# Linear attention and SwiGLU on one core: opening batch in token halves, row transposes by DMA, casts on ScalarE, loads in order of need

## The chip, the cores and the metric

The kernel runs on one core of a Trainium2 chip. The metric is the device time of the whole program in microseconds (us), as the median of several executions. A profile is one execution with the hardware profiler on. Its span runs from the first to the last instruction and is some 2 us shorter than the time.

Names of the engines in the profile: PE is TensorE's matmuls, PEld its weight loads, DVE is VectorE, ACT is ScalarE, POOL is GpSimd, SPq and ACTq are the sequencers of SyncE and ScalarE while they issue DMAs. PSUM is the memory in which the matmuls of these kernels leave their results.

## The reference, cut to what matters

```python
def _attn_ref(q, k, v, g_norm):                 # 8 batches, 8 heads, 576 tokens, 64 per head
    kv = np.einsum('bhsd,bhse->bhde', k, v)
    out = np.einsum('bhsd,bhde->bhse', q, kv)
    rms = np.sqrt(np.mean(out * out, axis=-1, keepdims=True) + 1e-06)
    return out / rms * g_norm

def _moe_ref(x, w_gate, w_val, w_out, rms_g):   # x: 4608 tokens x 512; d_ff = 1536
    rms = np.sqrt(np.mean(x * x, axis=-1, keepdims=True) + 1e-06)
    xn = x / rms * rms_g
    g = xn @ w_gate
    return (g / (1 + np.exp(-g)) * (xn @ w_val)) @ w_out
```

The first function feeds the second: its output, with the heads side by side, is `x`. The softmax is absent, so a whole batch needs only one 64x64 matrix per head, but all of K and V must have been seen before the first output exists.

## The kernel before

Both kernels work through nine groups of 512 tokens. Groups 0 to 7 are the first 512 tokens of each batch; group 8 holds the eight tails of 64 tokens. In a group there are 12 "up" units (four gate and four value matmuls of 128x512, then silu on ScalarE and the product `h` on VectorE) and four "down" units of 12 matmuls each. The attention of the next batch is put between these units by hand; the program order on each engine is the order in which the lines are issued.

Two normalisations are folded into one factor `alpha` per token and head. It needs two sums of squares per head, one plain and one weighted with the gains, and an inverse square root made by two Newton steps on VectorE ("the chain"). The gains go into the FFN weights when these are rounded to bf16.

The parts that the change touches:

```python
        def sums(self, c):                       # for each 128 tokens: VectorE
            nc.vector.tensor_tensor(out=wsq, in0=self.sq, in1=gsq8, op=OP.mult)
            nc.vector.reduce_sum(out=self.ssq[:, c, :], in_=self.sq, axis=AX.X)
            nc.vector.reduce_sum(out=self.wssq[:, c, :], in_=wsq, axis=AX.X)

        def xT(self, pair):                      # rows -> columns on TensorE, then a PSUM copy
            ...
                    nc.tensor.matmul(ps[:, j, i, :], lhsT=self.xna[2 * pair + i][:, 2 * j : 2 * j + 2, :],
                                     rhs=identity, is_transpose=True, ...)
            nc.vector.tensor_copy(out=xnts[self.n][:, :, 256 * pair : 256 * pair + 256], in_=...)
    ...
    round_main(0, "k", nc.gpsimd)                # the opening: all of batch 0 first
    round_main(0, "v", nc.vector)
    round_main(0, "q", nc.scalar)
    att = Att(0)
    att.kv(); att.qT(0); att.qT(1)               # (one call per line in the kernel)
    for c in range(T):
        att.o(c)
        att.sums(c)
    att.chain_a(); att.chain_b()
    ...                                          # scale, transpose
    for blk in range(NF // JB):
        load_w12(blk)
        round_w12(blk, "g", nc.gpsimd)
        round_w12(blk, "v", nc.gpsimd)
    ...
    for n in range(B + 1):
        ...
                12: [lambda: nxt.xT(0), lambda: nxt.scale(2), lambda: nxt.scale(3)],
                13: [lambda: nxt.xT(1)],
        for unit in range(NF + T):
            if unit < NF:
                ffn.up(unit)
                if n == 0 and unit == NF - 1:    # all of w_out is rounded before the first down unit
                    for blk in range(NF // JB):
                        round_wo(blk, nc.vector if blk % 2 else nc.scalar)
            else:
                ffn.down(unit - NF)
            for step in steps.get(unit, []):
                step()
```

Of the kernel before, what the change touches and what calls it, by code (L numbers as in the profile page):

```python
# [17 lines left out]
def kernel(  # L18
# [22 lines left out]
    HALF_B = B // 2  # L41
    NS = d_model // 128
    NF = d_ff // 128
    JB = 2
    assert TAIL == 64 and B * TAIL == MAIN and 2 * D == 128

    consts = ctx.enter_context(tc.tile_pool(name="consts", bufs=1))
    qkv_pool = ctx.enter_context(tc.tile_pool(name="qkv", bufs=2))
    stage_pool = ctx.enter_context(tc.tile_pool(name="stage", bufs=8))
    raw_pool = ctx.enter_context(tc.tile_pool(name="raw", bufs=3))  # L50
    qt_pool = ctx.enter_context(tc.tile_pool(name="qt", bufs=2))
    outa_pool = ctx.enter_context(tc.tile_pool(name="outa", bufs=6))
    sq_pool = ctx.enter_context(tc.tile_pool(name="sq", bufs=3))
    xna_pool = ctx.enter_context(tc.tile_pool(name="xna", bufs=4))
    stat_pool = ctx.enter_context(tc.tile_pool(name="stat", bufs=2))
    xnt_pool = ctx.enter_context(tc.tile_pool(name="xnt", bufs=2))
    h_pool = ctx.enter_context(tc.tile_pool(name="hsb", bufs=1))
    silu_pool = ctx.enter_context(tc.tile_pool(name="silu", bufs=3))
    osb_pool = ctx.enter_context(tc.tile_pool(name="osb", bufs=3))

    gps_pool = ctx.enter_context(tc.tile_pool(name="gps", bufs=2, space=bass.MemoryType.PSUM))
    vps_pool = ctx.enter_context(tc.tile_pool(name="vps", bufs=2, space=bass.MemoryType.PSUM))
    ops_pool = ctx.enter_context(tc.tile_pool(name="ops", bufs=2, space=bass.MemoryType.PSUM))
    att_pool = ctx.enter_context(tc.tile_pool(name="att", bufs=2, space=bass.MemoryType.PSUM))
# [4 lines left out]
    def main_view(x, b):  # L69
        return x[b, :, 0:MAIN, :].rearrange("h (p t) d -> p h (t d)", t=T)  # L70

    def tail_view(x, b0, b1):
        return x[b0:b1, :, MAIN:S, :].rearrange("b h r d -> r (b h) d")



    k_tail = consts.tile([128, HALF_B, H, D], BF16, name="k_tail")
    q_tail = consts.tile([128, HALF_B, H, D], BF16, name="q_tail")
    v_tail = consts.tile([128, B, H, D], BF16, name="v_tail")

    def load_tails(x, dst, b0, b1):
        u = b0 // HALF_B
        cols = slice(b0, b1) if dst is v_tail else slice(b0 - u * HALF_B, b1 - u * HALF_B)
        nc.gpsimd.dma_start(
            out=dst[u * TAIL : (u + 1) * TAIL, cols].rearrange("r b h d -> r (b h) d"),
            in_=tail_view(x, b0, b1),
        )

    batches = {}
    raws = {}  # L90

    def load_main(b):
        for name, src in (("k", k), ("v", v), ("q", q)):
            st = raw_pool.tile([128, H, T * D], FP32, name="raw")
            nc.sync.dma_start(out=st, in_=main_view(src, b))  # L95
            raws[b, name] = st

    def round_main(b, name, engine):
        t = qkv_pool.tile([128, T, H, D], BF16, name=name + "_t")
        for hh in range(2):  # L100
            hs = slice(hh * H // 2, (hh + 1) * H // 2)
            dst = t[:, :, hs, :].rearrange("p t h d -> p h t d")
            src = raws[b, name][:, hs, :].rearrange("p h (t d) -> p h t d", t=T)
            if engine is nc.scalar:
                engine.copy(out=dst, in_=src)
            else:
                engine.tensor_copy(out=dst, in_=src)  # L107
        batches.setdefault(b, {})[name] = t


    gcol = consts.tile([128, 1], FP32, name="gcol")
    gview = g_norm.rearrange("(d o) -> d o", o=1)
    nc.sync.dma_start(out=gcol[0:D], in_=gview)
    nc.sync.dma_start(out=gcol[D : 2 * D], in_=gview)
    rmsg_sb = consts.tile([128, NS], FP32, name="rmsg_sb")
    nc.sync.dma_start(out=rmsg_sb, in_=moe_rms_g.rearrange("(s p) -> p s", p=128))
    gnorm_bc = consts.tile([128, D], FP32, name="gnorm_bc")
    nc.sync.dma_start(out=gnorm_bc, in_=g_norm.partition_broadcast(128))

    load_main(0)  # L120
    nc.vector.memset(k_tail, 0.0)
    nc.vector.memset(v_tail, 0.0)
    load_tails(k, k_tail, 0, 1)
    load_tails(v, v_tail, 0, 1)

    identity = consts.tile([128, 128], BF16, name="identity")
    make_identity(nc, identity)

    kv_all = consts.tile([128, B, NS, 2, D], BF16, name="kv_all")
    nc.vector.memset(kv_all, 0.0)  # L130

    rowscale = consts.tile([128, NS], FP32, name="rowscale")
    nc.vector.tensor_scalar(
        out=rowscale, in0=rmsg_sb, scalar1=gcol[:, 0:1], scalar2=None, op0=OP.mult
    )
    gsq8 = consts.tile([128, H, D], BF16, name="gsq8")
    nc.vector.tensor_tensor(
        out=gsq8[:, 0, :], in0=gnorm_bc, in1=gnorm_bc, op=OP.mult
    )
    for n in (1, 2, 4):  # L140
        nc.vector.tensor_copy(out=gsq8[:, n : 2 * n, :], in_=gsq8[:, 0:n, :])

    qt_tail = consts.tile([128, HALF_B, 2, NS, 128], BF16, name="qt_tail")


    wg_sb = consts.tile([128, NS, d_ff], BF16, name="wg_sb")
    wv_sb = consts.tile([128, NS, d_ff], BF16, name="wv_sb")
    wo_sb = consts.tile([128, NF, d_model], BF16, name="wo_sb")
    wg_view = moe_w_gate.rearrange("(s p) f -> p s f", p=128)
# [3 lines left out]
    w_stages = {}  # L153

    def load_w12(blk):
        cols = slice(blk * JB * 128, (blk + 1) * JB * 128)
        for name, view in (("g", wg_view), ("v", wv_view)):
            st = stage_pool.tile([128, NS, JB * 128], FP32, name="w_st")
            nc.sync.dma_start(out=st, in_=view[:, :, cols])
            w_stages[name, blk] = st  # L160

    def round_w12(blk, name, engine):
        dst = {"g": wg_sb, "v": wv_sb}[name]
        for s in range(NS):
            engine.tensor_scalar(  # L165
                out=dst[:, s, blk * JB * 128 : (blk + 1) * JB * 128], in0=w_stages[name, blk][:, s, :],
                scalar1=rowscale[:, s : s + 1], scalar2=1.0, op0=OP.mult, op1=OP.mult,
            )

    def load_wo(blk):  # L170
        st = stage_pool.tile([128, JB, d_model], FP32, name="w_st")
        nc.sync.dma_start(out=st, in_=wo_view[:, blk * JB : (blk + 1) * JB, :])
        w_stages["o", blk] = st

    def round_wo(blk, engine):
        dst = wo_sb[:, blk * JB : (blk + 1) * JB, :]
        if engine is nc.scalar:
            engine.copy(out=dst, in_=w_stages["o", blk])  # L178
        else:
            engine.tensor_copy(out=dst, in_=w_stages["o", blk])  # L180


    xnts = {}

    class Att:



        def __init__(self, n):
            self.n = n  # L190
            self.tail = n == B

        def kv(self):
            n, t = self.n, batches[self.n]
            ps = att_pool.tile([128, NS, 2 * D], FP32, name="att_ps")
            for j in range(NS):
                for c in range(T + 1):
                    if c < T:
                        kk, vv = t["k"][:, c, 2 * j : 2 * j + 2, :], t["v"][:, c, 2 * j : 2 * j + 2, :]
                    else:  # L200
                        kk, vv = k_tail[:, n % HALF_B, 2 * j : 2 * j + 2, :], v_tail[:, n, 2 * j : 2 * j + 2, :]
                    nc.tensor.matmul(  # L202
                        ps[:, j, :], lhsT=kk, rhs=vv,
                        start=(j == 0 and c == 0), stop=(j == NS - 1 and c == T),
                    )
            nc.vector.tensor_copy(out=kv_all[0:D, n, :, 0, :], in_=ps[0:D, :, 0:D])
            nc.vector.tensor_copy(out=kv_all[D:128, n, :, 1, :], in_=ps[D:128, :, D : 2 * D])

        def qT(self, pair):
            ps = att_pool.tile([128, 2, NS, 128], BF16, name="att_ps")  # L210
            for i in range(2):
                c = 2 * pair + i
                for j in range(NS):
                    src = q_tail[:, c, 2 * j : 2 * j + 2, :] if self.tail else (
                        batches[self.n]["q"][:, c, 2 * j : 2 * j + 2, :])
                    nc.tensor.matmul(  # L216
                        ps[:, i, j, :], lhsT=src, rhs=identity, is_transpose=True,
                        start=(i == 0 and j == 0), stop=(i == 1 and j == NS - 1),
                    )
            if self.tail:  # L220
                for i in range(2):
# [81 lines left out]
        def xT(self, pair):  # L303
            if pair == 0:
                xnts[self.n] = xnt_pool.tile([128, NS, MAIN], BF16, name="xnt")
# [87 lines left out]
    for n in range(B + 1):  # L393
# [8 lines left out]
        if n + 2 < B:  # L402
            load_main(n + 2)
# [74 lines left out]
```

## Time and profile before

The median of the first three runs is 398.69 us (397.28 to 400.91). The best ruler for this kernel is the start of the first gate matmul of each group, read from the timeline of PE:

| stage (before) | from | to | us |
|---|---|---|---|
| opening | 0 | 41.84 | 41.8 |
| group 0 | 41.84 | 95.70 | 53.9 |
| group 1 | 95.70 | 136.56 | 40.9 |
| groups 2 to 7 | 136.56 | 362.39 | 225.8 |
| group 8 and the last stores | 362.39 | 398.2 | 35.8 |

(The prediction has 42.8 and 96.5 for the first two borders: the first gate matmuls of these groups stand apart from the next by a gap, 0.22 us in group 0, and I had cut after them.)

The page of the kernel before, parts 1 and 2: busy time of each engine, then PE's busy share and the granted TensorE clock in 40 slices of 10 us, each digit in tenths.

```profile
PE 331.8 (83%) x1868; PEld 167.0 (42%) x1904; DVE 208.5 (52%) x443; ACT 145.1 (36%) x247; POOL 81.0 (20%) x107
...
PE   0231890897998999899989998998999899989995
...
PEclk9999996896998999999989999999999999989999
```

PE is busy 83% of the span, and the first four slices hold little (9.15 us of the first 41.84, by the windows view): the opening is not bound by TensorE. The view of waits, PE's own: what it waited for, total, number of times, longest.

```profile
PE att_ps L309 <- DVE xna L298: 28.7, 18, 11.9
...
PE att_ps L202 <- DMA v_tail<-in_v_dram: 9.6, 1, 9.6
```

The longest of the first, 11.9 us, is the sums and the chain of the opening; the 9.6 us is one load in group 0. The timeline of PE (start, duration, engine, line, operation, output from inputs, array tile, size, count, and in brackets the idle time before with its releaser) shows that load, and the start of group 0:

```profile
41.84 0.58 PE L329 MATMUL g_ps<-xnt,wg_sb 128*128 128x512 bf16 x1 [0.78 <-DVE xnt L314]
...
43.51 1.91 PE L335 MATMUL v_ps<-xnt,wv_sb 128*128 128x512 bf16 x4
45.21 1.08 PE L329 MATMUL g_ps<-xnt,wg_sb 128*128 128x512 bf16 x4
...
69.02 0.27 PE L202 MATMUL att_ps<-v_tail,k_tail 128*128 128x128 bf16 x1 [9.56 <-DMA v_tail<-in_v_dram]
```

Finally the windows view for a steady group: the window, its length, then busy time and number of instructions of PE, PEld, DVE, ACT and POOL, the granted clock, the DMA share, GB/s.

```profile
212.45:249.57 37.12, 35.02 (x210) 17.83 (x212) 22.30 (x48) 15.25 (x26) 6.08 (x6) 1.00 0.35 115
```

Of 37.12 us PE is busy 35.0, and 35.0 is more than the 31.1 us that the FFN's 144 matmuls of 0.216 us need: attention and its transposes take the rest.

### The profile page before, as it was taken

What the parts mean: (1) busy time and instruction counts of PE and PEld (TensorE: products, weight loads), DVE (VectorE), ACT (ScalarE), POOL (GpSimd) and SP (SyncE); (2) the same over time, 40 slices, a digit from 0 to 9 for tenths busy, and PEclk for the clock granted to TensorE, in tenths of its full rate; (3) what the DMA queues carried; (4) which work ended last, traced back from release to release, by engine and by line L of the source; (5) the groups of instructions that cost most, each with busy time, mean ns of one, the idle gap of its engine ahead of it and who ended that gap; (6) DMA issues with size and microseconds to landing.
All of it is one profiled execution on the core that took longest, in us unless ns stands there. A gap on an engine that the chain in (4) does not pass through costs nothing.

```text
span 398.2 us, 4990 instructions
## 1 busy us (share of the span) xinstructions
PE 331.8 (83%) x1868; PEld 167.0 (42%) x1904; DVE 208.5 (52%) x443; ACT 145.1 (36%) x247; POOL 81.0 (20%) x107
## 2 busy tenths in 40 slices
PE   0231890897998999899989998998999899989995
PEld 0220440543543454355435544543454345434442
DVE  5268330395568157716852784388257815761320
ACT  1170130561551265136413631462255136412321
POOL 2299945600500032005100500050000000000000
PEclk9999996896998999999989999999999999989999
DMA  5999999817400290057005701740110020002004
GB/s 143 344 348 348 365 247 213 53 54 225 146 0 0 95 323 8 0 172 251 2 24 173 228 1 54 239 132 0 68 39 1 2 105 2 0 2 105 0 14 93
DMA packets 49145, 45.97 MB, mean 115 GB/s; under 512 B 14305, under 2 KB 45025, under 8 KB 49121
## 3 DMA queue, kind: packets, MB, share of 16 engines
q1 hardware_dynamic: 36704, 44.08, 34.5%
q0 software_dynamic: 12416, 1.57, 6.1%
q8 instruction: 15, 0.25, 0.2%
q14 instruction: 10, 0.07, 0.1%
HBM read 37.78 MB, written 9.44 MB: 119 GB/s over the span
## 4 chain that ended last, share of the span: by engine, by line
PE 63%; DVE 15%; DMA 9%; POOL 7%; issue 3%; SPq 2%; ACT 1%; DVEq 0%; ACTq 0%; POOLq 0%
PE o_ps L346 19%; PE v_ps L335 18%; PE g_ps L329 18%; DMA v_tail<-in_v_dram 6%; DVE h_sb L341 4%; POOL wg_sb L165 3%; POOL wv_sb L165 3%; DMA w_st<-in_moe_w_gate_dram 3%; DVE xna L298 3%; PE att_ps L202 2%; PE att_ps L309 2%; PE att_ps L243 2%; PE att_ps L216 2%; DVE ssq L257 1%; SPq L95 1%
## 5 line engine op out<-in xcount | busy, mean ns | idle before, releaser
L341 DVE TENSOR_TENSOR h_sb<-silu,v_ps 128x512 bf16<-128x512 bf16 x108 | 73.9, 685 | 123.3 <-PE v_ps L335 117.6
L329 PE MATMUL g_ps<-xnt,wg_sb 128*128 128x512 bf16 x414 | 111.2, 385 | 2.6 <-DVE xnt L314 1.6
L335 PE MATMUL v_ps<-xnt,wv_sb 128*128 128x512 bf16 x425 | 112.0, 384 | 0.6
L346 PE MATMUL o_ps<-wo_sb,h_sb 128*128 128x512 bf16 x421 | 101.8, 393 | 1.9 <-ACT wo_sb L178 1.3
L340 ACT ACTIVATE silu<-g_ps 128x512 bf16<-128x512 f32 x108 | 65.2, 603 | 103.3 <-PE g_ps L329 97.1
L335 PEld LDWEIGHTS <-wv_sb 128*128 128x128 bf16 x432 | 42.7, 99 | 52.7 <-issue 2.7
L346 PEld LDWEIGHTS <-h_sb 128*128 128x128 bf16 x432 | 42.8, 101 | 52.2 <-issue 8.1
L352 ACT COPY o_sb<-o_ps 128x512 f32<-128x512 f32 x36 | 21.1, 586 | 102.6 <-PE o_ps L346 102.4
L329 PEld LDWEIGHTS <-wg_sb 128*128 128x128 bf16 x432 | 40.8, 99 | 41.7 <-issue 4.1
L107 POOL CAST k_t<-raw 128x1024 bf16<-128x1024 f32 x16 | 16.5, 1062 | 160.9 <-DMA raw<-in_k_dram 123.3
L309 PE MATMUL att_ps<-identity,xna 128*128 128x128 bf16 x144 | 14.7, 240 | 28.7 <-DVE xna L298 28.7
L248 ACT ACTIVATE sq<-att_ps 128x512 bf16<-128x512 f32 x36 | 21.8, 605 | 14.0 <-PE att_ps L243 14.0
L309 PEld LDWEIGHTS <-xna 128*128 128x128 bf16 x144 | 9.6, 105 | 37.3 <-DVE xna L298 35.5
L202 PE MATMUL att_ps<-v_t,k_t 128*128 128x128 bf16 x128 | 11.6, 239 | 15.5 <-DVE v_t L107 15.5
L257 DVE TENSOR_REDUCE ssq<-sq 128x8 f32<-128x512 bf16 x36 | 24.4, 677 | 0.0
L258 DVE TENSOR_REDUCE wssq<-wsq 128x8 f32<-128x512 bf16 x36 | 24.3, 674 | 0.0
L314 DVE COPY xnt<-att_ps 128x1024 bf16<-128x1024 bf16 x18 | 12.4, 691 | 18.0 <-PE att_ps L309 17.9
L250 ACT CAST outa<-att_ps 128x512 bf16<-128x512 f32 x36 | 21.2, 588 | 0.0
L228 ACT COPY qt<-att_ps 128x1024 bf16<-128x1024 bf16 x16 | 16.1, 1013 | 11.4 <-PE att_ps L216 11.4
L256 DVE TENSOR_TENSOR wsq<-sq,gsq_137 128x512 bf16<-128x512 bf16 x36 | 17.1, 476 | 5.2 <-ACT sq L248 5.2
L202 PEld LDWEIGHTS <-k_t 128*128 128x128 bf16 x128 | 10.1, 108 | 21.0 <-POOL k_t L107 12.4
L107 POOL CAST q_t<-raw 128x1024 bf16<-128x1024 f32 x14 | 14.2, 1045 | 7.5 <-DMA raw<-in_q_dram 5.0
(85 smaller groups left out, 192.8 us busy)
## 6 DMA issues: line engine op xcount, KB each, us to landing
raw<-in_k_dram SPq DMA_DIRECT2D x8, 1024.0 KB, 7.1
raw<-in_v_dram SPq DMA_DIRECT2D x8, 1024.0 KB, 9.6
raw<-in_q_dram SPq DMA_DIRECT2D x8, 1024.0 KB, 11.7
out_dram<-o_sb SPq DMA_DIRECT2D x16, 512.0 KB, 2.9
w_st<-in_moe_w_gate_dram SPq DMA_DIRECT2D x6, 512.0 KB, 8.9
w_st<-in_moe_w_val_dram SPq DMA_DIRECT2D x6, 512.0 KB, 8.8
w_st<-in_moe_w_out_dram SPq DMA_DIRECT2D x6, 512.0 KB, 10.3
out_dram<-o_sb SPq DMA_DIRECT2D x8, 128.0 KB, 2.3
```

The costliest lines, as they stand in the source:

```text
L107: engine.tensor_copy(out=dst, in_=src)
L165: engine.tensor_scalar(out=dst[:, s, blk * JB * 128 : (blk + 1) * JB * 128], in0=w_stages[name, blk][:, s, :], scalar1=rowscale[:, s : s + ...
L202: nc.tensor.matmul(ps[:, j, :], lhsT=kk, rhs=vv, start=(j == 0 and c == 0), stop=(j == NS - 1 and c == T),)
L248: nc.scalar.activation(out=sq, in_=ps, func=ACT.Square)
L257: nc.vector.reduce_sum(out=self.ssq[:, c, :], in_=self.sq, axis=AX.X)
L258: nc.vector.reduce_sum(out=self.wssq[:, c, :], in_=wsq, axis=AX.X)
L309: nc.tensor.matmul(ps[:, j, i, :], lhsT=self.xna[2 * pair + i][:, 2 * j : 2 * j + 2, :], rhs=identity, is_transpose=True, start=(i == 0 an ...
L329: nc.tensor.matmul(g_ps, lhsT=wg_sb[:, s, j * 128 : (j + 1) * 128], rhs=x[:, s, :], start=(s == 0), stop=(s == NS - 1),)
L335: nc.tensor.matmul(v_ps, lhsT=wv_sb[:, s, j * 128 : (j + 1) * 128], rhs=x[:, s, :], start=(s == 0), stop=(s == NS - 1),)
L340: nc.scalar.activation(out=silu, in_=g_ps, func=ACT.Silu)
L341: nc.vector.tensor_tensor(out=self.h[:, j, :], in0=silu, in1=v_ps, op=OP.mult)
L346: nc.tensor.matmul(o_ps, lhsT=self.h[:, j, c * 128 : (c + 1) * 128], rhs=wo_sb[:, j, :], start=(j == 0), stop=(j == NF - 1),)
```

## The change

Its intent: the opening should reach the FFN sooner, and a steady group should hold fewer TensorE instructions and no wait for the rows of the next group.

- Batch 0 is worked in two halves of 256 tokens. Its sums of squares are small matmuls against a four-column matrix `sel` (a plain and a weighted sum for each of two heads), and its chain has 12 operations, not 16. Group 0 starts on the first half.
- The transposes of `q` and of the normalised rows, from batch and group 2 on, are `dma_start_transpose` on SyncE's queue; they were TensorE matmuls plus PSUM copies. Batch 1 keeps TensorE.
- The casts to bf16 in steady groups go from GpSimd to ScalarE; the weight rounding from GpSimd to ScalarE (gate) and VectorE (value).
- The tails of K and V are plain loads with a cast, no longer casting DMAs of GpSimd. Loads are issued in the order of need; seven stage buffers are shared.
- The rounding of `w_out` moves into the down part of group 0, block by block.

The diff cut to its core (cuts marked):

```diff
+    def chain(u, w, nc_, name):                 # 11 operations, and one before it
+        ...
+        nc.vector.scalar_tensor_tensor(out=z, in0=m.to_broadcast(shape), scalar=eps, in1=u, ...)
+        ...
+        def x_rows(self, c):
+            nc.sync.dma_start_transpose(
+                out=xnts[self.n][:, :, 128 * c : 128 * c + 128],
+                in_=self.xna[c].rearrange("p h d -> p (h d)"),
+            )
...
-    round_main(0, "k", nc.gpsimd)
-    round_main(0, "v", nc.vector)
-    round_main(0, "q", nc.scalar)
-    att = Att(0)
-    ...
+    A, Bh = Open(0), Open(1)                    # the two halves
+    for j in range(NS):                         # per pair of heads
+        cast_piece(0, "k", j, nc.vector)
+        cast_piece(0, "v", j, nc.scalar)
+        ps = att_pool.tile([128, 128], FP32, name="att_ps")
+        warm(ps, 3, 128)                        # three dummy matmuls
+        for c in range(T + 1):
+            nc.tensor.matmul(ps, lhsT=kbs[0][:, c, hs, :], rhs=vbs[0][:, c, hs, :], ...)
+        nc.vector.tensor_copy(out=kv_all[0:D, 0, j, 0:D], in_=ps[0:D, 0:D])
+        nc.vector.tensor_copy(out=kv_all[D:128, 0, j, D:128], in_=ps[D:128, D:128])
+        A.outT(j)                               # one matmul of 128x256
+        A.square(j)                             # ScalarE
+    A.sums(); A.o(); ...; A.chain(); ...        # (one call per line in the kernel)
+    ffn.up(0, 0, 256)
+    Bh.chain()
+    ...
+    ffn.up(3, 0, 256)
+    for j in range(4):
+        ffn.up(j, 256, 512)                     # the second half of units 0 to 3
+        ...
+    for j in range(4, NF):
+        ffn.up(j)
+        ...
+    att.kv_products((0, 1))                     # batch 1, in the down part of group 0
+    att.kv_products((2, 3))
+    att.kv_copy()
+    for blk in range(3):
+        round_wo(blk, 0, nc.scalar)
+        round_wo(blk, 1, nc.vector)
+        if blk == 0:
+            for i in range(4):
+                cast_piece(1, "q", i, nc.scalar if i % 2 else nc.vector)
+        for c in range(2):
+            ffn.down_products(c, 4 * blk, 4 * blk + 4)
+        if blk == 0:
+            att.q_turn(0, nc.scalar)
+        if blk == 1:
+            att.q_turn(1, nc.vector)
+            att.o(0)
+            att.sums(0)
+        if blk == 2:
+            att.o(1)
+            att.sums(1)
+    ...
+    ffn.down_products(3, 0, NF)
+    att.x_turn(0, nc.vector)
+    att.x_turn(1, nc.vector)
+    ffn.down_out(3)
+    for n in range(1, B + 1):                   # the other groups
+        ...
```

## The prediction

> **What bounds the kernel now.** The span is 398.2 us. In the chain of waits TensorE (PE) has 63%. The windows view, cut at the first gate matmul of each token group: opening with group 0, 96.5 us; group 1, 40.0; groups 2 to 7, 37.1 to 38.8 (226.0 together); tail group 8 with the last stores, 35.7.
> In the first 42.8 us PE is busy only 9.9 us. The timeline shows why: K, V, Q land at 11.3, 14.7, 17.7 us; all of batch 0 is finished before the first FFN matmul; sums and the Newton chain keep VectorE from 23 to about 37 us; GpSimd rounds weights until 43.8. Then PE waits 9.6 us for v_tail (waits view), a cast DMA behind GpSimd work.
> A steady group is 31.1 us of FFN (144 matmuls of 0.216 us), 1.1 K^T V, 0.9 q transposes, 0.9 output, 0.9 x transposes, and 1.5 to 1.9 of PE waiting for xna (13.3 us in the waits of 96.5 to 362.5).
>
> **What the change does.**
> 1. Opening. Halves of 256 tokens; sums become small matmuls; the chain has 12 operations, not 16; rounding is split over ScalarE and VectorE; tails are plain loads; loads come in order of need. At the 345 GB/s seen before, batch 0 (3.25 MB) lands by about 13 us, the first weights by 16 to 20. Casts, squares, chain (12 x 0.21), scale and transposes put the first FFN matmul at about 23 us (42.8 before). Group 0 stays partly starved to about 35 us (second half's chain, rounding), and its end is VectorE work (batch 1's sums, chain, scale: about 17 us). Group 1 starts at about 66 us instead of 96.5: saves 30.
> 2. Steady groups. DMA transposes remove 1.8 us of PE transposes and the xna wait, and free the PSUM copies (2 x 1.01 us ScalarE, 2 x 0.69 VectorE). The whole chain now precedes the last h multiply: an estimated 0.5 us of PE. Groups 2 to 7: 33.8 us instead of 37.7, saving 23.
> 3. ScalarE gets the casts: 14 x about 0.6 us in the four down units, with four output copies about 10.8 us against 10.4 of PE. It runs about 2 us late; two gate banks should absorb that.
> 4. Group 1 has its own casts right after batch 2 is loaded: about 35. Tail group 35.
> Sum: 66 + 35 + 203 + 35 = 339 us.
>
> **The risky step** is the DMA transpose (eight of 128x512 per group, on SyncE's queue); this trace has none. The Trainium skill, "DMA: Bandwidth & Descriptors", section on latency and other measured facts, gives 261 GB/s, so 128 KB is an estimated 0.5 us; "VectorE: DVE Perf Modes", the three transpose paths, gives 1.31 us for one 128x128. If four such blocks went serially, that is about 5 us per 128x512 and 42 us per group: DMA would bound the groups (about 400 us in all). I expect 1 to 2 us each. From the last scale to the next gate matmul there are about 5 us, so a wait of 0 to 1 us there is included.
>
> **Predicted:** 339 us, range 322 to 362. Faster by over 2%: 0.92; within 2%: 0.04; slower: 0.04.
>
> **What would show it.** Right: first gate matmul at 20 to 27 us; group 1's at 60 to 72; groups of 33 to 35 us, clock near 1.0; no long PE waits on xnt or qt. Wrong: gate matmuls waiting for xnt's DMA at each group start; silu late at group starts with ScalarE full; PE waiting on VectorE between 25 and 35 us much longer, or on weight loads held by seven stage buffers.

## The result, and the profile after

The median after is 372.06 us (four runs, 370.68 to 373.2), against 399.8 us of four runs of the kernel before. The ratio is 0.9325, with a 95% interval of 0.9269 to 0.9382. Ratios here are the mean time of one kernel's fast runs over that of the other's of the same rounds, so they are not quite the ratios of the medians quoted. The four of before lie within 1.1% of each other. Executions over 1.5% slower than the fastest of the same kernel are left out of the means. The kernel is faster, but by 7%, not by the 15% that were predicted, and 372 lies above the range of 322 to 362.

The same ruler, the first gate matmul of each group, in the kernel after:

| stage | before, us | predicted, us | after, us |
|---|---|---|---|
| opening | 41.8 | 23 | 29.5 |
| group 0 | 53.9 | 43 | 60.9 |
| group 1 | 40.9 | 35 | 39.7 |
| groups 2 to 7 | 225.8 | 203 | 204.5 |
| group 8 | 35.8 | 35 | 35.7 |
| sum (span) | 398.2 | 339 | 370.3 |

The steady groups came as predicted. The miss is 24.4 us before group 1 starts (90.4 instead of 66), 4.7 in group 1, 1.5 in groups 2 to 7, 0.7 in group 8. The last 1.8 us are the difference of time and span, which the sum ignored: 24.4 + 4.7 + 1.5 + 0.7 + 1.8 = 33.1.

Group 0 became longer than before, although a wait of 9.56 us that it contained is gone. The page of the kernel after, parts 1 and 2 (slices of 9.3 us):

```profile
PE 325.9 (88%) x1717; PEld 161.6 (44%) x1749; DVE 192.3 (52%) x439; ACT 189.3 (51%) x349; POOL 8.7 (2%) x18
...
PE   0567997586989799999999999999999999999995
...
PEclk9999998887899989999999999999999999999999
```

There are dips in PE's row and in its clock between 56 and 102 us. The waits of PE:

```profile
PE o_ps L333 <- ACT wo_sb L95: 5.5, 3, 2.1
...
PE g_ps L321 <- DMA xnt<-xna: 2.9, 1, 2.9
PE o_ps L333 <- DVE h_sb L327: 2.8, 6, 0.5
```

The first line is new: three waits of PE for the rounding of `w_out` on ScalarE. The timeline of PE, from the first gate matmul to the start of group 1 (a line that holds several matmuls tells their spacing: the distance to the next line over the count):

```profile
29.46 1.06 PE L321 MATMUL g_ps<-xnt,wg_sb 128*128 128x256 bf16 x4
30.32 1.06 PE L321 MATMUL v_ps<-xnt,wv_sb 128*128 128x256 bf16 x4
...
57.79 0.39 PE L219 MATMUL att_ps<-vb,kb 128*128 128x128 bf16 x4
59.47 1.07 PE L219 MATMUL att_ps<-vb,kb 128*128 128x128 bf16 x16 [1.29 <-DVE kb L97]
61.94 3.25 PE L333 MATMUL o_ps<-wo_sb,h_sb 128*128 128x512 bf16 x8 [1.40 <-ACT wo_sb L95]
65.02 0.61 PE L243 MATMUL att_ps<-identity,qb 128*128 128x128 bf16 x8
67.67 3.15 PE L333 MATMUL o_ps<-wo_sb,h_sb 128*128 128x512 bf16 x7 [2.04 <-ACT wo_sb L95]
...
74.01 0.59 PE L333 MATMUL o_ps<-wo_sb,h_sb 128*128 128x512 bf16 x2 [2.10 <-ACT wo_sb L95]
...
87.16 0.40 PE L301 MATMUL att_ps<-identity,xna 128*128 128x128 bf16 x4 [2.05 <-DVE xna L283]
...
90.36 1.86 PE L321 MATMUL g_ps<-xnt,wg_sb 128*128 128x512 bf16 x4 [0.78 <-DVE xnt L97]
```

Two things are to be seen. First, the waits in brackets. Second, the spacing: at 61.94 us eight 128x512 matmuls take 3.08 us, 0.385 each, where a steady group has 0.216 (a line may show one fewer, x7 for 8: some records are missing in a trace). The half-width matmuls at 29.46 us take 0.86 us for four, 0.215 each; those after 41 us, not shown, 0.109. It is the same instruction at half and at full rate. The windows view confirms it for the down part of group 0 and shows a steady group for comparison:

```profile
57.80:90.36 32.56, 20.72 (x116) 10.50 (x116) 17.53 (x40) 12.54 (x21) 0.00 (x0) 0.82 0.31 99
198.98:232.70 33.72, 33.10 (x178) 16.02 (x180) 19.07 (x41) 20.72 (x40) 3.60 (x2) 1.00 0.55 164
```

The down part took 32.56 us, with PE busy for 20.72, at a mean clock of 0.82. Its work at full rate is about 14 us (48 matmuls of 0.216 us are 10.4; the durations under the prediction's first heading add 1.1 for K^T V and 0.9 each for `q` transposes, outputs and row transposes). In the steady group PE is busy 33.10 of 33.72 us, with 178 instructions where there were 210.

### The profile page after: what moved, and what is told of

Same layout as the page of the kernel before. It is cut to its first block, busy times and chain, and to the rows that moved or that the text cites. A ratio compares the mean times of both kernels' runs of the same rounds, so it can differ in the third digit from the quotient of the medians.

```text
span 370.3 us, 4813 instructions
## 1 busy us (share of the span) xinstructions
PE 325.9 (88%) x1717; PEld 161.6 (44%) x1749; DVE 192.3 (52%) x439; ACT 189.3 (51%) x349; POOL 8.7 (2%) x18
## 4 chain that ended last, share of the span: by engine, by line
PE 58%; DVE 11%; ACT 3%; issue 2%; SPq 2%; DMA 1%; DVEq 0%
PE v_ps L321 19%; PE g_ps L321 19%; PE o_ps L333 16%; DVE h_sb L327 3%; PE att_ps L258 2%; PE att_ps L219 2%; SPq L651 1%; DVE ssq L273 1%; ACT o_sb L341 1%; DVE sa L190 1%; DVE sc L192 1%; ACT vb L95 1%; DVE wsq L272 1%; ACT kb L95 1%; DVE sr L174 1%
## 5 line engine op out<-in xcount | busy, mean ns | idle before, releaser
L327 DVE TENSOR_TENSOR h_sb<-silu,v_ps 128x512 bf16<-128x512 bf16 (+1 forms) x112 | 74.6, 666 | 129.7 <-PE v_ps L321 79.2
L321 PE MATMUL g_ps<-xnt,wg_sb 128*128 128x512 bf16 (+1 forms) x428 | 113.7, 385 | 4.3 <-DMA xnt<-xna 2.9
L321 PE MATMUL v_ps<-xnt,wv_sb 128*128 128x512 bf16 (+1 forms) x446 | 114.9, 381 | 0.5
L326 ACT ACTIVATE silu<-g_ps 128x512 bf16<-128x512 f32 (+1 forms) x112 | 65.6, 586 | 76.9 <-PE g_ps L321 71.6
L283 DVE TENSOR_TENSOR xna<-outa,sy 128x512 bf16<-128x512 bf16 x32 | 19.9, 685 | 0.1
L95 ACT CAST vb<-st 128x512 bf16<-128x512 f32 x32 | 18.5, 615 | 0.0
L272 DVE TENSOR_TENSOR wsq<-sq,gsq 128x512 bf16<-128x512 bf16 x32 | 13.4, 419 | 4.3 <-ACT sq L263 4.3
L95 ACT CAST qb<-st 128x512 bf16<-128x512 f32 x26 | 14.3, 618 | 1.7 <-DMA st<-in_q_dram 1.7
L258 PE MATMUL att_ps<-kv_all,qt 128*128 128x128 bf16 x112 | 11.2, 226 | 0.0
L95 ACT CAST kb<-st 128x512 bf16<-128x512 f32 x20 | 10.9, 619 | 0.0
```

Source lines behind the costliest of these rows:

```text
L95: engine.copy(out=dst, in_=src)
L258: nc.tensor.matmul(ps[:, 2 * j : 2 * j + 2, :], lhsT=a, rhs=b, start=(j == 0 and i == 0), stop=(j == NS - 1 and i == len(terms) - 1),)
L283: nc.vector.tensor_tensor(out=self.xna[c], in0=self.outa[c], in1=self.alpha[:, c, :].to_broadcast([128, H, D]), op=OP.mult)
L321: nc.tensor.matmul(ps[:, 0:w], lhsT=wt[:, s, j * 128 : (j + 1) * 128], rhs=x[:, s, lo:hi], start=(s == 0), stop=(s == NS - 1),)
L326: nc.scalar.activation(out=silu[:, 0:w], in_=g_ps[:, 0:w], func=ACT.Silu)
L327: nc.vector.tensor_tensor(out=self.h[:, j, lo:hi], in0=silu[:, 0:w], in1=v_ps[:, 0:w], op=OP.mult)
```

## The experiments

All outputs were correct. A ratio is to the kernel before of the same rounds. The borders of the groups come from the one profiled run of each kernel.

My theory after reading the traces: group 0 loses its time to (a) waits in program order, PE to ScalarE to PE, for the rounding of `w_out`, and (b) half rate of TensorE that follows such gaps. The rivals: the loss is in the tail of VectorE work of batch 1 (sums, chain, scale), or in the DMA.

### e3_wo: the rounding of w_out out of the ping-pong

```diff
+    for blk in range(3):
+        round_wo(blk, 0, nc.scalar)
+        round_wo(blk, 1, nc.vector)
     att.kv_products((0, 1))
     att.kv_products((2, 3))
     att.kv_copy()
+    for i in range(4):
+        cast_piece(1, "q", i, nc.scalar if i % 2 else nc.vector)
     for blk in range(3):
-        round_wo(blk, 0, nc.scalar)
-        round_wo(blk, 1, nc.vector)
-        if blk == 0:
-            for i in range(4):
-                cast_piece(1, "q", i, nc.scalar if i % 2 else nc.vector)
         for c in range(2):
```

> Group 0's down part took 30 us (60.3 to 90.4 us) for about 14 us of TensorE work. Here all six roundings of w_out stand before the K^T V product of batch 1 on ScalarE and VectorE, so that no down product waits for a rounding queued behind a copy that waits for TensorE. TensorE's program is the same. Theory W (waits in program order are the cause and the half clock follows from them): the waits on wo_sb (5.7 us) go, the down products run at 0.216 us, not 0.43, and group 1 starts 6 to 9 us earlier. Rival C (half clock is there by itself): group 1 starts 3 to 5 us earlier and the down products stay at 0.43 us.

Measured: 362.18 us (360.12 to 362.86), ratio 0.9108 (0.9039 to 0.9177). Group 0 fell from 60.9 to 50.5 us; the groups after it kept their lengths. The timeline of PE of this kernel:

```profile
59.74 1.89 PE L333 MATMUL o_ps<-wo_sb,h_sb 128*128 128x512 bf16 x8
...
76.65 0.40 PE L301 MATMUL att_ps<-identity,xna 128*128 128x128 bf16 x4 [2.05 <-DVE xna L283]
...
77.85 1.21 PE L301 MATMUL att_ps<-identity,xna 128*128 128x128 bf16 x8 [0.21 <-DVE xna L283]
```

The three blocks of `w_out` products now run without their waits, at 0.216 us per matmul. Only 5.8 us of waiting was taken away (1.40 + 2.04 + 2.10 + 0.24), and 0.57 came back as a wait for the cast of `q`; the rest of the 10.4 us is rate: by the windows view PE was busy for 16.11 us of the down part, with the same matmuls, where it had been busy for 20.72. Why did the second block wait in the kernel after? On ScalarE the copy of the transposed `q` stands ahead of the rounding of block 1, and that copy waits for TensorE's transposes, which stand behind the products of block 0. ScalarE was idle for 2.74 us until the copy began at 65.67 us, and the rounding began at 66.58. So TensorE waits for ScalarE, which had waited for TensorE. It is a wait for the order of two queues, not for work. As for the DMA, no wait of PE in group 0 is put down to one, and none of ScalarE or VectorE between 29.5 and 90.4 us either, so that rival is out.

The wait for `xna` of 2.05 us at the end of group 0 stays: this is the VectorE tail (the rival's share). And half rate comes back at 77.85 us (eight transposes in 1.21 us; four in 0.40 at 76.65), after 3.25 us (74.60 to 77.85) in which TensorE did only two short batches of transposes: group 1 still begins at half rate.

### e4_warm: dummies in the gaps, all waits left as they are

```diff
+    def keep_warm(count):
+        warm(gps_pool.tile([128, MAIN], FP32, name="g_ps"), count)
     ...
     for blk in range(3):
         ...
+        keep_warm(16)
         for c in range(2):
             ffn.down_products(c, 4 * blk, 4 * blk + 4)
     ...
+    keep_warm(16)
     att.x_turn(0, nc.vector)
```

> The other half of the pair: the waits of group 0's down part stay, but 16 matmuls without use (128x256) stand in TensorE's program before each of the three down blocks and before the x transposes, so that TensorE is busy in its gaps. Theory C (half clock after the gaps costs much): down products run at 0.216 us, the start of group 1 too, and the total falls by 5 to 7 us. Theory W alone (only the waits matter): the total changes by less than 2 us, or rises.

Measured: 364.47 us (362.87 to 367.04), ratio 0.9181 (0.9102 to 0.9259). The dummies write a bank that nobody reads; they fill time in which TensorE would wait anyway.

```profile
61.28 1.89 PE L333 MATMUL o_ps<-wo_sb,h_sb 128*128 128x512 bf16 x8
...
65.66 1.89 PE L333 MATMUL o_ps<-wo_sb,h_sb 128*128 128x512 bf16 x8 [0.30 <-ACT wo_sb L95]
...
85.09 1.02 PE L321 MATMUL g_ps<-xnt,wg_sb 128*128 128x512 bf16 x4 [0.80 <-DVE xnt L97]
```

The products at 61.28 us run at full rate (eight in 1.73 us; 3.08 in the kernel after). Group 0 lasted 55.5 us (5.4 less), group 1 37.2 (2.5 less: its first twelve matmuls were not at half rate), group 2 33.7 (1.4 less). The profiled span fell from 370.3 to 361.8. Extra work made the kernel faster, with each dependency as it was: so half rate alone cost several us. Not all of the 8.5 us is the dummies' doing: 1.0 arose in the up part, before the first of them (it took 27.4 us, 28.3 in the kernel after), and 1.4 in group 2. The down part of group 0 gave 4.4 and group 1 2.5. The ratios of the two kernels, each to its own runs of before, say 5.7 us (0.9325 - 0.9181, of 399). I take some 6. e3 and e4 remove overlapping parts, so their gains must not be added.

In group 2 no dummies stand, and its wait of 2.89 us for the rows was still there; only its first matmuls now ran at full rate. That says that it was the rate, and that there is some luck in when the rate changes.

### e2_pipe: the pairs of the opening one step ahead

In the loop over the four pairs of heads, each engine waits for another once per step. The timeline of the kernel after, PE and ScalarE, for one pass:

```profile
12.43 0.69 PE L516 MATMUL att_ps<-vb,kb 128*128 128x128 bf16 x5 [1.96 <-ACT vb L95]
...
13.67 0.39 PE L453 MATMUL g_ps<-qt,kv_all 128*128 128x256 bf16 x1 [0.55 <-DVE kv_all L520]
...
14.10 0.38 ACT L459 ACTIVATE sqT<-g_ps 128x256 bf16<-128x256 f32 x1 [1.73 <-PE g_ps L453]
...
14.38 0.61 ACT L95 CAST vb<-st 128x512 bf16<-128x512 f32 x1
15.04 0.48 PE L516 MATMUL att_ps<-vb,kb 128*128 128x128 bf16 x3 [0.66 <-ACT vb L95]
```

ScalarE's cast of the next `v` stands behind the square of this pair, which waits for this pair's output: 2.61 us per pass, four times. The edit casts the next pair first and issues the output matmul and the square one pass later.

```diff
+    kv_in(0)                                    # k on VectorE, v on ScalarE, as before
     for j in range(NS):
-        cast_piece(0, "k", j, nc.vector)
-        cast_piece(0, "v", j, nc.scalar)
+        if j + 1 < NS:
+            kv_in(j + 1)
         ...
-        A.outT(j)
-        A.square(j)
+        if j > 0:
+            A.outT(j - 1)
+            A.square(j - 1)
```

> Undoes the ping-pong of the opening: the K and V casts of the next head pair are issued ahead of the copies and squares of the one before; nothing else. In the changed kernel each of the four head pairs takes 2.61 us (cast on ScalarE, product, two copies, output, square, then the next cast). Theory O (the opening is late because engines in program order wait for each other): a pair takes about 1.2 us, the first gate matmul comes 4 to 5 us earlier than 29.5 us, and the total falls by 3 to 5 us. Rival (the opening is bound by the arrival of its loads): the first gate matmul moves by less than 1.5 us.

Measured: 368.77 us (368.49 to 369.0), ratio 0.9282 (0.922 to 0.9344); the interval overlaps that of the kernel after, and the profile decides. The timeline of PE:

```profile
16.62 0.71 PE L522 MATMUL att_ps<-vb,kb 128*128 128x128 bf16 x5 [1.78 <-DVE kb L97]
...
25.85 1.06 PE L321 MATMUL g_ps<-xnt,wg_sb 128*128 128x256 bf16 x4
```

The first gate matmul stands at 25.85 us, 3.6 earlier (4 to 5 had been expected); group 0 kept its length (61.1). So 3.6 of the 6.5 us by which the opening was late were this ping-pong. What then holds the fourth pair (the line at 16.62 us) is its cast of `k`: on VectorE it stands behind a cast of the second half's `q`, whose load comes late.

### e1_gam: the gains later in the queue

The opening's longest PE wait, 7.7 us for the gains' load, stands at the head of TensorE's queue. The edit moves the transpose of the gains, with its four VectorE instructions, from ahead of the casts of `q` to behind the casts of the tails.

```diff
-    gam_ps = att_pool.tile([128, 8], FP32, name="att_ps")
-    nc.tensor.matmul(gam_ps[:, 0:5], lhsT=gam[0:5, :], rhs=ident32[0:5, 0:5], is_transpose=True, ...)
-    ...
     alloc_q(0)
     ...
     cast_tail(0, "v", nc.scalar)
+    gam_ps = ...                                # the same lines here
```

> The small transpose of the gains and the three VectorE operations that follow it stand first in TensorE's and VectorE's programs and wait for a GpSimd-issued load until 7.7 us, with the casts of q behind them; here they are moved behind the q casts and transposes of the first half. If this queue order delays the opening, the q casts start at about 5.5 us instead of 8.6, and the first gate matmul comes 1 to 2.5 us earlier. If the loads of k and v bound it, it moves by less than 0.7 us.

Measured: 371.6 us (369.31 to 372.56), ratio 0.9323 (0.9264 to 0.9381). The first gate matmul moved from 29.46 to 29.07 us, 0.4; kernels with the same opening as the kernel after had it anywhere between 29.29 (e5) and 30.16 us (e10), so this is hardly a gain. The casts of `q` did begin earlier, but the first cast of `k` then waited 2.00 us for its load until 11.27 us: here the opening hangs on the loads. A long wait that stands first in the list was worth 0.4 us at most.

### e6_openwarm: more dummies in the opening

```diff
-        warm(ps, 3, 128)
+        warm(ps, 10, 128)
     ...
+    ps = att_pool.tile([128, 256], FP32, name="att_ps")
+    warm(ps, 4)
     for j in range(NS):
         Bh.outT(j)
     ...
+    warm(ops_pool.tile([128, d_model], FP32, name="o_ps"), 12)
     Bh.rows((nc.vector, nc.scalar))
```

> Matmuls without use fill TensorE's gaps in the opening (10 instead of 3 before each K^T V product, 4 before the second half's outputs, 12 before its x transposes). In the changed kernel matmuls ran at half rate until 40.9 us, also the 40 half-width ones after 29.5 us (0.213 us each). Theory C: full rate comes at 20 us or before, the first gate matmul about 1.5 us and the end of group 0's up part 4 to 6 us earlier. Rival: half rate there follows from something else (width 256, weight loads), and the up part ends within 1.5 us of where it did.

Measured: 369.15 us (366.35 to 371.44), ratio 0.9262 (0.918 to 0.9343). The expectation of full rate by 20 us failed: the windows view of the opening and the timeline of PE where the rate at last changes:

```profile
10.57:30.09 19.52, 14.90 (x122) 11.81 (x121) 10.78 (x40) 9.78 (x23) 0.00 (x0) 1.00 0.98 344
```

```profile
31.80 0.87 PE L321 MATMUL g_ps<-xnt,wg_sb 128*128 128x256 bf16 x4
32.50 0.60 PE L321 MATMUL v_ps<-xnt,wv_sb 128*128 128x256 bf16 x4
```

PE was busy 14.90 of 19.52 us (76%), and the small matmuls stayed at half rate until about 32.3 us. The first gate matmul came 0.6 us later, which is within the spread given under e1. Group 0 was 5.0 us shorter in the profiled run; part of that is that the down part happened to stay at full rate until about 70 us, so I don't book it to the dummies. Which condition was missing is open: each pass still has gaps of 0.55 us, and some of the busy time was transposes (see the last section).

### e11_full: group 0 without halves

```diff
-    ffn.up(0, 0, 256)
     Bh.chain()
     ...
-    ffn.up(1, 0, 256)
     Bh.rows((nc.vector, nc.scalar))
     ...
-    ffn.up(2, 0, 256)
-    ffn.up(3, 0, 256)
     for j in range(4):
-        ffn.up(j, 256, 512)
+        ffn.up(j)
```

All casts, chains and roundings keep their order; units 0 to 3 are full-width.

> Undoes the token halves in group 0's up part only: the first four units run at full width, after both halves of batch 0 are normalised; the opening before is the same. If halves pay, the two half units that ran in the shadow of the second half's chain (3.4 us of TensorE) are lost and the end of the up part comes 2 to 4 us later. Rival: they only fill time at half rate, VectorE starts the second half's chain earlier without them, and the up part ends within 1.5 us of 57.8.

Measured: 371.6 us (370.66 to 372.5), ratio 0.9333 (0.9286 to 0.9379). The timeline of PE:

```profile
34.99 0.59 PE L321 MATMUL g_ps<-xnt,wg_sb 128*128 128x512 bf16 x1 [0.67 <-ACT xnt L95]
...
57.82 0.39 PE L219 MATMUL att_ps<-vb,kb 128*128 128x128 bf16 x4
```

The first gate matmul comes 5.5 us later than in the kernel after, and the up part ends at 57.82 us where it ended at 57.79: starting on the first half paid nothing here. The half units ran at half rate, and they put the second half's chain behind the products of the first on VectorE and ScalarE. Whether halves pay where they run at full rate, as in e9, no run shows.

### e5_xrows: the store behind the transposes

At the start of group 2 PE waits 2.90 us for the last transposed rows. In SyncE's queue a store of the output (0.53 us) stands between the second and the third transpose. The theory: this order costs the wait. The edit issues transposes 3 and 4 one unit earlier.

```diff
             steps[12] += [nxt.chain, ..., lambda: nxt.scale(1), lambda: nxt.x_rows(1)]
-            steps[13] += [lambda: nxt.scale(2), lambda: nxt.x_rows(2), ...]
+            steps[12] += [lambda: nxt.scale(2), lambda: nxt.x_rows(2), ...]
```

> Group 1 only: the DMA transposes of x rows 2 and 3 are issued before the store of the first output pair instead of after it, as in the later groups. In the changed kernel they wait on SyncE's queue behind that store, which waits for an output copy behind ScalarE's casts; TensorE waits 2.9 us for xnt and then runs 7 matmuls at half clock. If that order is the cause, the wait goes and the total falls by 3 to 5 us. If the transposes themselves are slow, the wait stays.

Measured: median 371.29 us of four runs (366.17 to 372.68); two of them slow, so there is no ratio from the times. The timelines of SyncE's sequencer and of PE, first after, then e5:

```profile
123.18 2.50 SPq L290 DMA_TRANSPOSE xnt<-xna  x2
...
126.40 2.54 SPq L290 DMA_TRANSPOSE xnt<-xna  x2
...
130.10 1.89 PE L321 MATMUL g_ps<-xnt,wg_sb 128*128 128x512 bf16 x4 [2.90 <-DMA xnt<-xna]
```

```profile
120.43 5.12 SPq L290 DMA_TRANSPOSE xnt<-xna  x4
...
126.73 1.70 PE L321 MATMUL g_ps<-xnt,wg_sb 128*128 128x512 bf16 x4 [2.27 <-DMA xnt<-xna]
```

The wait only fell from 2.90 to 2.27 us: the theory fell. In both kernels the four transposes are issued one after another at some 1.25 to 1.28 us each, and the last lands some 2.4 us after its issue began. What makes them late is the chain: it starts on VectorE at unit 12 of 16 in this group, because its attention steps sit at units 7 to 11, and the scaling that writes `xna` begins at 122.42 us in the kernel after, 5 us before TensorE runs out of work.

### e10_g1turn: TensorE turns the rows of group 2

```diff
-            steps[12] += [nxt.chain, lambda: nxt.scale(0), lambda: nxt.x_rows(0), ...]
-            steps[13] += [lambda: nxt.scale(2), lambda: nxt.x_rows(2), ...]
+            steps[12] += [nxt.chain] + [lambda c=c: nxt.scale(c) for c in range(T)]
+            steps[14] += [lambda: nxt.x_turn(0, nc.vector), lambda: nxt.x_turn(1, nc.vector)]
```

> Group 1 only, after e5_xrows showed that the store in SyncE's queue cost just 0.5 us: there the four transposes are issued one after another, 1.25 us each, from when VectorE has the first xna row, 4 us before the group's last matmul, and the last lands 2.3 us after its issue. Here x of batch 2 is transposed on TensorE before the last down product instead. If late xna plus serial issue is the cause, the 2.9 us wait at the start of group 2 goes and so do its matmuls at half rate; groups 1 and 2 together fall from 74.9 to 71 to 72.5 us, and the total by 2.5 to 4 us. If not, they stay above 74.

Measured: 369.31 us (368.51 to 369.79), ratio 0.9266 (0.9228 to 0.9304). Groups 1 and 2 together fell from 74.88 to 71.32 us. The timeline of PE:

```profile
125.19 1.06 PE L301 MATMUL att_ps<-identity,xna 128*128 128x128 bf16 x16
126.09 2.75 PE L333 MATMUL o_ps<-wo_sb,h_sb 128*128 128x512 bf16 x11
128.68 1.03 PE L321 MATMUL g_ps<-xnt,wg_sb 128*128 128x512 bf16 x4
```

All 16 transposes take 0.9 us of TensorE between the products of group 1's down units, and group 2 starts without a wait and at full rate. Where the rows come late, the path with the shorter delay is the better one, though it takes time of TensorE.

### e7_peturn and e7b_peturn: TensorE transposes back in every group

```diff
+                steps[0] += [lambda: nxt.q_turn(0, nc.scalar)]
+                steps[3] += [lambda: nxt.q_turn(1, nc.scalar)]
             ...
-                steps[11] += [lambda c=c: nxt.scale(c), lambda c=c: nxt.x_rows(c)]
-                steps[12] += [lambda c=c: nxt.scale(2 + c), lambda c=c: nxt.x_rows(2 + c)]
+            steps[11] += [lambda: nxt.scale(0), lambda: nxt.scale(1)]
+            steps[12] += [lambda: nxt.x_turn(0, nc.vector), lambda: nxt.scale(2), lambda: nxt.scale(3)]
+            steps[13] += [lambda: nxt.x_turn(1, nc.vector)]
```

The four DMA transposes of `q` of each steady group (`later.q_rows`) are removed too.

> Undoes the DMA transposes in groups 2 to 7 alone: q and x are transposed on TensorE with copies from PSUM, as in the kernel before. If the DMA transposes are what shortened the groups from 37.1 to 33.7 us, they are 36.5 to 37.5 us again (1.8 us of transposes and 1.5 to 2 us of waiting for xna) and the total rises by about 17 to 22 us. If the gain came from elsewhere (casts off GpSimd, shorter chain), the groups stay under 35 us.

Measured: the three fast runs gave 384.32, 385.54 and 385.89 us, ratio 0.9674 (0.961 to 0.9738). The fourth, which is the profiled one, took 460.18 us at a granted clock of 0.759: a slow run, whose profile can't be compared.

> The same kernel as e7_peturn, for a profile in the fast state (that of e7_peturn fell in the slow one, while its fast runs took 385 us, 13.5 more than the changed kernel's 371.5). Groups 2 to 7 should then be about 36.0 us, by the total. Of the 2.3 us more per group, 1.8 should be the TensorE transposes (16 at 0.056 us twice) and the rest waiting for xna; if the wait is over 1 us, groups are over 36.5.

Measured: one run, 384.59 us; it agrees with the three fast ones. The windows view of a steady group, to be held against those of before and after above:

```profile
202.58:238.87 36.29, 35.19 (x210) 17.78 (x213) 20.51 (x43) 22.80 (x42) 3.60 (x2) 1.00 0.38 124
```

Groups 3 to 6 last 36.28 us, 2.55 more than with DMA transposes, and less than the 37.12 of the kernel before; the 0.84 that remain belong to the other parts of the change (the shorter chain, the PSUM copies' place, the casts), which I have not taken apart. In the waits of PE the line for the transposes waiting for `xna` has 16 waits and 4.7 us, against 4 waits and 2.6 us in the kernel after: twelve short ones came back, 2.1 us over all groups. The bulk of the 2.55 us per group is the transposes themselves (two kinds of 0.9 us, that is 1.8).

### e8_poolcast: the steady casts on GpSimd again

```diff
-                    steps[u].append(lambda b=b, item=item: do_cast(b, item, nc.scalar))
+                    steps[u].append(lambda b=b, item=item: do_cast(b, item, nc.gpsimd))
```

> Undoes the ScalarE rounding in groups 2 to 7 alone: the fourteen casts of a batch go to GpSimd, as before, at the same places. ScalarE was expected to be just able to hold them, so I expect groups of 33.4 to 34.2 us, the same as 33.7, and the total within 2 us of the changed kernel's. If rounding on ScalarE is a gain by itself (VectorE slower beside GpSimd), groups take over 34.7 us.

Measured: 374.42, 375.0, 375.36 and 368.81 us. The first three were slow, being more than 1.5% above the last, and the profile is of such a run. In it three of the groups 3 to 6 last 34.04 to 34.94 us, and PE's waits for `h_sb` are 4.8 us in all, with 1.7 the longest (2.8 and 0.5 in the kernel after). I read from this only that no gain of GpSimd showed; whether ScalarE is better stays open.

One thing about GpSimd stands in the trace of before, and I had passed over it: in the opening, while GpSimd rounded weights (until 43.8 us), most of the 16 operations of VectorE's chain took 0.42 us each (31.1 to 36.1 us); operations of the same size take 0.19 us in its other groups and in the kernel after. So a part of what the opening gained may come from taking the rounding off GpSimd, and not from the four operations fewer. No run separates the two.

### e9_best: what helped, together

The edits of e2_pipe, e3_wo and e10_g1turn; the last two dummy groups of e6_openwarm, without those in the pair loop; dummies around the last transposes of group 0; and the load of batch 2 ahead of the casts of batch 1's tails.

```diff
+    load_batch(2)
     cast_tail(1, "k", nc.vector)
     ...
-    load_batch(2)
     ffn.down_products(3, 0, NF)
+    warm(gps_pool.tile([128, MAIN], FP32, name="g_ps"), 16)
     att.x_turn(0, nc.vector)
     att.x_turn(1, nc.vector)
+    warm(gps_pool.tile([128, MAIN], FP32, name="g_ps"), 6)
```

> A version meant to beat both: the pipelined opening (e2_pipe), w_out rounded ahead (e3_wo), x of batch 2 transposed on TensorE (e10_g1turn), batch 2 loaded before the down part of group 0, and matmuls without use in the gaps that remain (second half's rows, before and after x of batch 1). If the terms add: first gate matmul at 26 us, group 1 at about 75, groups 1 and 2 together 70, the rest as in the changed kernel: a total of 352 to 357 us. If the gains overlap, 358 to 361, no better than e3_wo.

Measured: 351.96 us (six runs, 350.73 to 352.39), ratio 0.8827 (0.8796 to 0.8857). It beats both kernels: some 46 us under before, 20 under after. The borders: first gate 25.8, group 1 at 74.0, groups 1 and 2 together 69.0, groups 3 to 6 33.7 each. The page's part 1, and the timeline of PE at the first gate matmul and at the start of group 1:

```profile
PE 316.2 (91%) x1762; PEld 159.6 (46%) x1794; DVE 193.3 (55%) x441; ACT 188.8 (54%) x349; POOL 8.7 (2%) x18
```

```profile
25.77 0.60 PE L321 MATMUL g_ps<-xnt,wg_sb 128*128 128x256 bf16 x4
26.20 0.60 PE L321 MATMUL v_ps<-xnt,wv_sb 128*128 128x256 bf16 x4
...
73.99 1.02 PE L321 MATMUL g_ps<-xnt,wg_sb 128*128 128x512 bf16 x3
```

PE is busy 91%, and both lines are at full rate (0.109 and 0.216 us of spacing); the clock of the profiled run was 0.999. Here, other than in e6, full rate had come by 25.8 us.

## Why the prediction was wrong

1. "Batch 0 lands by about 13 us ... the first FFN matmul at about 23 us": 29.5. The operations were costed one by one, but in each pass of the pair loop they stand in a ring through three engines: 2.61 us per pass. e2 shows that 3.6 of the 6.5 us were this ring. The rest is not isolated. The small matmuls at half rate are part of it by their spacing; e1 shows that the order of the gains' load is hardly (0.4 us, within the spread).

2. The failing step is "Group 0 stays partly starved to about 35 us ..., and its end is VectorE work ... Group 1 starts at about 66 us". It started at 90.4. Given the first gate at 29.5, group 0 took 60.9 us where 43 had been allowed. Two terms were missing. The first is waits by program order in the down part: 11.7 us of waiting in its 32.6 us, of which 5.8 for the rounding of `w_out`. The second is a clock at half rate, which the prediction did not mention for this stage: e4 shows some 6 us for it, with the waits in place (4.4 in the down part of group 0 and 2.5 in group 1 by the borders, 5.7 by the ratios). With the rounding ahead (e3), group 0 falls by 10.4 us. The VectorE work that the prediction did name was real but the smaller part: 2.05 us of waiting for `xna` remain in e3.

   That leaves 7.5 of the 17.9 us by which group 0 was longer than allowed, and no run isolates them. The up part is where to look: it took 28.3 us in the kernel after, for 96 matmuls that at 0.216 us are 20.7. In it stand some 40 half-width matmuls at half rate (40 x 0.106 = 4.2 us) and a wait of 2.27 us for the second half's rows.

   Both terms could have been had from the material before the run. The new order of `round_wo`, `q_turn` and `down_products` is in the diff, and the trace of before shows half rate after its own long gap: at 43.51 us four value matmuls take 1.70 us, 0.43 each.

3. The halves of the opening batch were counted as a gain. e11 shows none at the half rate at which they ran: the up part ends at the same time without them (57.82 and 57.79 us).

4. "Group 1 ... about 35": 39.7. Its first twelve matmuls ran at half rate (12 x 0.21 = 2.5 us), and at its end stands the wait of 2.9 us for the DMA transposes. I had allowed 0 to 1 us there, on "about 5 us from the last scale to the next gate matmul", which holds for a steady group. In group 1 the chain is issued later. e5 and e10 show that the late chain and the four serial transposes make this wait, not the store in the queue.

5. The steady groups were right, and for the stated reasons: 33.73 us (33.8 predicted); PE waits for `h_sb` six times, 0.47 us each (0.5 estimated), and for no transposed rows. e7b shows 2.55 us per group for the DMA transposes. The risky step, DMA transposes at 5 us each, did not come: the line of DMA issues in the page gives the time from issue to landing.

```profile
xnt<-xna SPq DMA_TRANSPOSE x28, 2.4
```

On SyncE's sequencer each takes 1.25 us; eight per group make some 10 us of 33.7.

6. "ScalarE ... about 2 us late; two gate banks should absorb that" held: PE shows no wait for silu in the steady groups. Whether ScalarE was needed for the casts is open (e8). Group 8 was right (35.7 for 35).

The program of group 0 is the same in several of these kernels, and its length in their profiles was 60.9, 60.4, 60.9, 60.9, 59.1 and 58.2 us (after, e1, e10, e8, e7b, e5). So differences of 1 or 2 us in group 0 mean nothing; the 5.4 and 10.4 us of e4 and e3 do, and the times agree with them in kind (medians 7.6 and 9.9 us below the kernel after; by the ratios 5.7 and 8.7).

## What to carry to other kernels

When work is split finely between engines, read the program order of each queue as a ring: the time per pass is the sum around the ring, and an idle engine with its data present is no help if an earlier line in its queue waits. Cost a gap on TensorE twice, as time and as half rate afterwards, until the matmul spacing proves otherwise; filling gaps with dummy matmuls was worth some 6 us here, removing half of the waiting 9 to 10. An asynchronous DMA transpose pays where its rows are ready some 6 us ahead of need (worked out: three issues of 1.25 us, and 2.4 us for the last one to land), and where they are not, TensorE's 0.9 us is cheaper.

## What the Trainium skill lacked or had wrong

- "TensorE: Matmul & The Clock Gate", Part 1: The HAM clock gate, says that TensorE starts at half rate, goes to full after about 3.4 us of sustained work, falls back after an idle window of that length, and that the moment varies. The runs agree in kind: 0.43 against 0.216 us for a 128x512 matmul. The closing section, Why this matters for your kernels, asks for no gaps over about 3 us. In these runs shorter ones were enough: after idle gaps of 1.29 and 1.40 us with 1.07 us of work between them (58.2 to 61.9 us) the kernel after was at half rate, and again after the gap of 2.04 us. The page's "A second HAM failure mode" does say that frequent short idles between groups of matmuls make the clock fall back, but gives no length. These runs give no rule either: a wait of 2.9 us at the start of group 2 was followed by half rate in the kernel after (130.10 us) and by full rate in e4 (122.33 us); and in the opening e6, with TensorE busy for 76%, was at half rate until 32.3 us, while e9, busy for 63% (10.57 to 25.30 us), was at full rate by 25.8.
- The same page, Part 4: PE-mode transpose, says that transposes don't count as busy in the same way for this gate. That would help to explain the falls at 67.67 us (a gap of 2.04 us after 0.61 us of transposes) and in e3 (3.25 us of gaps and transposes), and the failure of e6 (76% busy for 19.5 us without full rate). Against it, e4 kept full rate through 3.3 us of gaps and transposes (81.8 to 85.1 us). No run here separates the two; the page gives no busy share that is needed either.
- No page says that a profile's granted clock reads 1.00 in the opening while TensorE is at half rate: the windows view of e6 has 1.00 for 10.57 to 30.09 us, where the four 128x256 dummies at 25.16 us were 0.22 us apart (0.109 in the up part, after 41 us). The spacing has to be read there. The Clock Gate page does warn that the trace events of the gate can be unreliable.
- "VectorE: DVE Perf Modes", The three transpose paths, has 1.31 us for a 128x128 by DMA and 390 ns by TensorE. Here a 128x512 transpose between on-chip buffers took about 1.25 us of its queue and landed after 2.4 us, so four blocks did not cost four times the figure; and TensorE's were 0.056 us apart in a stream (16 in 0.9 us, e10).
- "DMA: Bandwidth & Descriptors", Latency and other measured facts, gives 261 GB/s for DMA transposes. The four of group 1 moved 128 KB each in 1.28 us of issue, some 100 GB/s (worked out from e5's 5.12 us for four): the issues stand end to end, so the issue time of the queue bounds them. No page gives that time for this chip by name: a table of the same page has sequencer cycles of a DMA transpose for "previous generations", for other sizes.
